# Moving a matmul kernel's squares, weight steps and first products between engines and slots

## The chip, the cores and the metric

One core of one Trainium2 chip runs the whole kernel as one launch. The metric is device time in microseconds (us), from the start to the end of one execution; the kernel before is shown with the median of three runs. The profile is of one execution. Its engines are PE (TensorE's matmuls), PEld (its weight loads), DVE (VectorE), ACT (ScalarE), POOL (GpSimd) and SP (SyncE, which issues the transfers here). Each engine works through its own queue in order; between engines there are only semaphores.

## The reference

Three layers, one behind the other: attention over a local window and a few global positions, a soft mixture of eight experts, and a feed-forward layer whose activation is a squared relu.

```python
def _attn_ref(q, k, v, n_global, n_local):        # batch 4, heads 8, sequence 768, head size 64
    ...
    scores = np.where(keep, scores, -1000000000.0)  # local window or global position
    ...
    return np.matmul(a, v)

def _moe_ref(x, phi, w1, w2):                      # 3072 tokens, width 512, 8 experts of 4 slots
    logits = x @ phi
    d = softmax over tokens; slot_input = d.T @ x
    for e in range(E):
        slot_out[e] = np.maximum(slot_input[e] @ w1[e], 0.0) @ w2[e]
    c = softmax over slots
    return c @ slot_out

def _moe2_ref(x, w_in, w_out):                     # 512 -> 2048 -> 512
    r = np.maximum(x @ w_in, 0.0)
    return (r * r) @ w_out
```

(The two softmax lines stand in words; the reference subtracts the maximum, takes exp and divides by the sum.)

## The kernel before

**Order.** The program is written with a manual schedule: every engine runs its instructions in the order in which the code emits them, so moving a line of code moves the instruction in its engine's queue. The file's names `V`, `G`, `nc.scalar`, `nc.tensor` and `nc.sync` are DVE, POOL, ACT, PE and SP. A tile with `bufs=2` is a ring of two buffers: the third user waits until the first is read. PSUM tiles are banks of 128x512 float32, and a wait on one is for the whole bank. `warm(n, ...)` issues n small matmuls whose result nobody reads.

**Stages.** Attention and routing run in units until about 172 us. The tail of routing (L714 to L796) works on the last two chunks of tokens, K and L: it updates the running sums `rden` and `acc`, turns the last weights (`pd`, copied to `db`), and ends with `slotZ`, the input of the experts. `w1_of` (L819) and `w2_of` (L923) stream the experts' weights through PE, the latter into one bank `pSO`. Between the experts `spread_T` and `spread_ev` (L884 to L889) turn a quarter of the combine weights `c_tok` on PE and store it by ACT and DVE in `cst`, in two halves. Then `pSO` is copied to `SO`, turned (`pst`, `soT`) and multiplied by the first part of w_in (`pu`, L1293), which gives `U0`: the tokens' combine and w_in are one product from here on, `cst` x `U`.

**The feed-forward layer.** The 2048 inner columns come in five parts of WIDTHS = 256, 384, 384, 512, 512, counted q = 0 to 4, and the 3072 tokens in ND = 6 blocks of 512, counted d. For parts 0 to 3 one loop goes over q, d and four steps m, each step the place of one block of 128 output rows; k = 4d + m counts the 24 steps of a part. A step emits, in this order: a number of background steps for the next part's weights, one first product `h` of the next block with its `gate` (L1055, L1043 to L1049), and the second products of this block (L1075, L1076, L1084), whose sum DVE adds into the output accumulator (L1089). A second product needs a high and a low part of the square: `gate` takes the relu on ACT (L1043), the exact square, by DVE from the bank or, with `own`, by ACT from the relu (L1045 or L1047), the rounded square on ACT (L1048) and their difference, the low part, on POOL (L1049; on DVE for the last block of q = 3). Its tile `rg` is on the ring of two `e`, the `h` banks on the rings `h` and `k` of two.

**Background steps.** They convert float64 words of the weights to float32 (L932 on ACT, L933, L934 and L937 on DVE), multiply w_in by the experts' sum (`make_u`, L1016 and L1024), and for the last part (`conv_last`) make seven sums of blocks with their high parts on ACT (L1002) and low parts on DVE and POOL (L1008). `total` and `room` (L1329) deal them out: for the last part `total` = 30 steps over `room` = 18 slots.

**The fifth part** (q = 4) forms pairs of blocks and multiplies them in seven products P1 to P7 (`pair`, L1208 to L1211) instead of eight. Its inner values y11, y12, y22 and y21 (`hy` on PE, `ry` = relu on ACT, squares `yt`), differences of them (L1161, DVE) and the high (ACT, L1148 or L1150) and low (POOL or DVE, L1156) parts `yop` are emitted by `y_steps` at slots of a table; slots below zero of the first pair fall into the steps k = 17 to 23 of q = 3, two each, and slot n from 0 on stands behind the n-th group of a pair. The products run as groups P1, P1, P5, P5, P6, P6, P3, P3, P7, P7 and so on, one per 128 rows.

**The start of the feed-forward layer** (`gemm1_first`): the first block's products for 256 tokens are made separately for the two halves k of the 256 columns, both in one bank, with warm matmuls behind them, then `gemm2_first` begins.

## Time and profile before

| | us |
|---|---|
| median of three runs (512.21, 512.89, 512.85) | 512.85 |
| the profiled execution, as timed | 513.21 |
| its span, first to last instruction | 511.4 |
| PE busy in the span (98%) | 500.3 |
| DVE busy (77%) | 391.9 |
| ACT busy (66%) | 335.3 |
| POOL busy (31%) | 158.1 |

The mean granted clock of TensorE is 0.999 of full speed. A row of the timeline shows an instruction's start, its duration, the line, the tiles (out<-in), and in brackets how long the engine was idle before it and what ended that. The rows of successive matmuls overlap: a 128x512 matmul is shown with 0.39 us while the next starts 0.23 us behind it, so PE's busy share says little about short waits, and starts are to be compared.

### The profile page before, as it was taken

Reading aid. Unit: us, or ns where it says so; the run is one execution under the profiler, and the core shown is the slowest. Engines: PE = TensorE matmul, PEld = TensorE weight load, DVE = VectorE, ACT = ScalarE, POOL = GpSimd, SP = SyncE. Lnnn points to the kernel's source line nnn. Section 1 sums busy time; section 2 is a strip of 40 time slices with the busy share of each in tenths; the row PEclk is TensorE's granted clock in tenths of the full one; section 3 lists DMA queues with packets and bytes.
Section 4 is the critical chain, followed back from the end, with each engine's and each line's share of the span. In section 5 each row is a group of like instructions: output and inputs, shape, how many; then the busy total and the mean of one; then the engine's idle time right before and its main releaser. Section 6 shows DMA issues by size and latency. Waiting matters only on the chain.

```text
span 511.4 us, 9819 instructions
## 1 busy us (share of the span) xinstructions
PE 500.3 (98%) x3517; PEld 382.0 (75%) x3517; DVE 391.9 (77%) x925; ACT 335.3 (66%) x840; POOL 158.1 (31%) x126
## 2 busy tenths in 40 slices
PE   9999999999999999999999999999999998999997
PEld 6777777687777744487887888788887876878785
DVE  7788888787887745688864765788696998579894
ACT  6987877878878402387985856576654566656650
POOL 7000000000000110000454554446644452866691
PEclk9999999999999999999999999999999999999999
DMA  8888999999994799913304040402200000013124
GB/s 278 261 283 295 365 309 326 313 330 314 318 336 139 274 357 420 406 64 126 123 1 164 1 164 2 164 2 67 97 1 1 2 0 1 1 41 124 62 104 164
DMA packets 25975, 86.93 MB, mean 170 GB/s; under 512 B 2882, under 2 KB 5442, under 8 KB 23746
## 3 DMA queue, kind: packets, MB, share of 16 engines
q1 hardware_dynamic: 25776, 86.13, 47.0%
q8 instruction: 29, 0.48, 0.4%
q14 instruction: 24, 0.20, 0.1%
q10 hardware_dynamic: 146, 0.13, 0.1%
HBM read 79.95 MB, written 6.29 MB: 169 GB/s over the span
## 4 chain that ended last, share of the span: by engine, by line
PE 53%; DVE 8%; ACT 1%; issue 0%; DVEq 0%; ACTq 0%
PE acc L1075 10%; PE acc L1076 10%; PE acc L1084 10%; PE pSO L923 3%; PE h L1055 3%; DVE rg L1047 1%; PE b2P L1211 1%; PE b2P L1208 1%; PE b2P L1209 1%; PE b1P L1211 1%; PE b0P L1211 1%; DVE oacc_p L1089 1%; PE b1P L1208 1%; PE b0P L1208 1%; PE b1P L1209 1%; PE b0P L1209 1%
## 5 line engine op out<-in xcount | busy, mean ns | idle before, releaser
L1075 PE MATMUL acc<-g,w 128*128 128x512 f32 x280 | 109.1, 390 | 0.0
L1076 PE MATMUL acc<-g,w 128*128 128x512 f32 x280 | 109.0, 389 | 0.0
L1049 POOL TENSOR_TENSOR g<-rg,g 128x512 fp32r<-128x512 f32 x56 | 75.4, 1352 | 81.8 <-DVE rg L1047 26.5
L263 ACT ACTIVATE sm<-sm,nm 128x256 f32<-128x256 f32 (+1 forms) x192 | 92.7, 487 | 1.3 <-DVE nm L248 1.3
L1084 PE MATMUL acc<-g,w 128*128 128x512 f32 x280 | 75.5, 389 | 0.0
L1043 ACT ACTIVATE rg<-h 128x512 f32<-128x512 f32 (+1 forms) x73 | 43.1, 591 | 44.0 <-PE h L1055 33.9
L248 DVE CUSTOM_DVE_ANT_0 sm<-s,mask 128x256 f32<-128x256 f32 (+1 forms) x192 | 66.8, 397 | 1.9 <-ACT sm L263 1.2
L1076 PEld LDWEIGHTS acc<-g,w 128*128 128x128 f32 x280 | 52.6, 188 | 11.0
L1084 PEld LDWEIGHTS acc<-g,w 128*128 128x128 f32 x280 | 52.6, 188 | 11.0
L1075 PEld LDWEIGHTS acc<-g,w 128*128 128x128 f32 x280 | 52.6, 188 | 10.7
L235 PE MATMUL s<-raw 64*128 64x256 f32 (+1 forms) x384 | 52.9, 397 | 0.0
L1089 DVE TENSOR_TENSOR oacc_p<-acc,oacc_p 128x512 f32<-128x512 f32 x48 | 32.4, 686 | 22.7 <-PE acc L1084 22.7
L673 POOL TENSOR_TENSOR lh<-lh 128x256 f32<-128x256 f32 x1 | 0.7, 731 | 158.4 <-PE pt L274 158.4
L1156 POOL TENSOR_TENSOR yop<-yt,yop 128x512 fp32r<-128x512 f32 x24 | 40.2, 1701 | 25.2 <-ACT yop L1148 9.0
L274 PE MATMUL pt<-con,sm 128*128 128x128 f32 x352 | 45.5, 277 | 1.6 <-ACT pT L280 1.6
L1048 ACT ACTIVATE g<-rg 128x512 fp32r<-128x512 f32 (+1 forms) x73 | 45.4, 621 | 1.6
L291 PE MATMUL o<-pT,v 128*64 128x128 f32 x704 | 44.2, 276 | 0.0
L274 PEld LDWEIGHTS pt<-con,sm 128*128 128x128 f32 x352 | 38.6, 141 | 7.3 <-ACT pT L280 2.8
L291 PEld LDWEIGHTS o<-pT,v 128*64 128x64 f32 x704 | 37.9, 137 | 6.9 <-ACT sm L263 2.1
L235 PEld LDWEIGHTS s<-raw 64*128 64x128 f32 x384 | 32.1, 194 | 14.6 <-DMA v<-in_vx 6.8
L1047 DVE SCALAR_TENSOR_TENSOR rg<-h,rg 128x512 f32<-128x512 f32 (+1 forms) x49 | 32.9, 674 | 9.6 <-ACT rg L1043 9.5
L263 ACT ACTIVATION_READ_ACCUMULATOR sm<-sm,nm 128x1 f32 x192 | 37.0, 193 | 0.0
(289 smaller groups left out, 880.0 us busy)
## 6 DMA issues: line engine op xcount, KB each, us to landing
w<-in_w SPq DMA_DIRECT2D x40, 512.0 KB, 6.6
raw<-in_qk SPq DMA_DIRECT2D x32, 384.0 KB, 5.3
w<-in_w SPq DMA_DIRECT2D x5, 2048.0 KB, 10.0
v<-in_vx SPq DMA_DIRECT2D x32, 256.0 KB, 4.3
raw<-in_qk SPq DMA_DIRECT2D x16, 320.0 KB, 5.1
win<-in_w_in SPq DMA_DIRECT2D x2, 2048.0 KB, 7.9
wout<-in_w_out SPq DMA_DIRECT2D x2, 2048.0 KB, 8.0
out_x<-oacc_p SPq DMA_DIRECT2D x15, 256.0 KB, 2.0
```

Source lines behind the costliest of these rows:

```text
L235: nc.tensor.matmul(sc[hh][:, tt, 0:n, :], lhsT=r[r0 : r0 + D, tt, :], rhs=rhs, start=True, stop=True)
L248: V.tensor_tensor_reduce(out=sm[:, j, 0:n, :], in0=sc[hh][:, tt, 0:n, :], in1=m[:, 2:3, :] if n == 1 else m[:, 0:2, :], scale=-QK_SCALE, s ...
L263: nc.scalar.activation(sm[:, j, 0:n, :], sm[:, j, 0:n, :], AF.Exp, bias=nm[:, j : j + 1], scale=-1.0, accum_out=chunk_sums(i // NPR)[:, tt ...
L274: nc.tensor.transpose(pp[tt][:, hh, c, :], sm[:, 2 * tt + hh, c, :], ident)
L291: nc.tensor.matmul(o[hh * D : hh * D + D, tt, :], lhsT=v[:, c * 3 if tt == 0 else 1 + c, hh * D : hh * D + D], rhs=pT[:, 2 * tt + hh, c, : ...
L1043: nc.scalar.activation(r, ph, AF.Relu)
L1048: nc.scalar.activation(g2[:, 0, js, cs], r, AF.Square)
L1049: (low or (G if q else V)).tensor_tensor(g2[:, 1, js, cs], g, g2[:, 0, js, cs].bitcast(F32), op=ALU.subtract)
L1075: nc.tensor.matmul(pa, lhsT=whi[:, j, ms], rhs=ghi[:, j, :], start=j == 0, stop=False)
L1076: nc.tensor.matmul(pa, lhsT=wlo[:, j, ms], rhs=ghi[:, j, :], start=False, stop=False)
L1084: nc.tensor.matmul(pa, lhsT=whi[:, j, ms], rhs=glo[:, j, :], start=False, stop=j == J - 1)
L1156: eng.tensor_tensor(lo[:, c], yt[y][:, c], hi[:, c].bitcast(F32), op=ALU.subtract)
```

## The change

It has six places.

1. `gate` of the part q = 3 takes the exact square on ACT for the column blocks j > 0, as the parts 1 and 2 do: 18 instructions (three of four column blocks, six token blocks) leave DVE's queue for ACT's.
2. The 30 background steps for the last part are dealt over `room` = 16 slots, not 18.
3. In the fifth part P6's high part moves from slot 0 to -1 and its low part from slot 2 to 1.
4. The first block's two column halves get a bank each in `gemm1_first`.
5. `SO` is copied by ACT in one instruction; the transpositions of the last eighth of the combine weights (`pc3_1`) move from the stream of w2 to behind `pc3_0`, into the bank that `pSO` leaves.
6. In the routing tail, `rden`'s first update becomes two POOL instructions further ahead; the transpositions `pd` of chunk L and their copy come ahead of the warm matmuls and of the product `pr`; `ps` is copied by ACT.

```diff
--- before.py
+++ after.py
@@ -716,6 +716,8 @@
     nc.tensor.transpose(pd[:, 0:P], dT[:, 0:P], ident)
     db = post.tile([P, 4, NS], F32, tag="db", name=f"db{K}")
     nc.scalar.copy(db, pd[:, 0:P].rearrange("p (t s) -> p t s", s=NS))
+    G.tensor_tensor(rden, rden, foK, op=ALU.mult)
+    G.tensor_tensor(rden, rden, dnK, op=ALU.add)
     xbL = post.tile([P, 2, DM], F32, tag="xT", name=f"xb{L}", bufs=2)
     px = bank(f"px{L}_0", True)
     turned(px, xL, 0)
@@ -734,8 +736,6 @@
     pS = bank(f"pS{K}")
     for t in range(4):
         nc.tensor.matmul(pS[t * NS : t * NS + NS, :], lhsT=db[:, t, :], rhs=(xb9 if t < 2 else xbK)[:, t % 2, :], start=True, stop=True)
-    idle = bank("idle2")
-    warm(3, con, idle)
     mxL, nmL = small("rmaxL"), small("nmL")
     V.tensor_reduce(mxL, pq[:, 0:TB], axis=AX.X, op=ALU.max)
     V.scalar_tensor_tensor(nmL, mxL, -1.0, pm[:, 0:1], op0=ALU.mult, op1=ALU.min)
@@ -745,9 +745,15 @@
     nc.scalar.activation(foL, nmK, AF.Exp, bias=nmL, scale=-1.0)
     dT = post.tile([P, TB], F32, tag="dT", name=f"dT{L}")
     nc.scalar.activation(dT, pq[:, 0:TB], AF.Exp, bias=nmL, scale=1.0, accum_out=dnL)
-    V.scalar_tensor_tensor(rden, rden, foK, dnK, op0=ALU.mult, op1=ALU.add)
     V.tensor_tensor(rden, rden, foL, op=ALU.mult)
     V.scalar_tensor_tensor(acc, acc, foK, pS, op0=ALU.mult, op1=ALU.add)
+    pd = bank(f"pd{L}")
+    for t in halves:
+        nc.tensor.transpose(pd[:, t * NS : t * NS + NS], dT[0:NS, t * P : t * P + P], ident[0:NS, 0:NS])
+    idle = bank("idle2")
+    warm(3, con, idle)
+    db = post.tile([P, 4, NS], F32, tag="db", name=f"db{L}")
+    nc.scalar.copy(db[:, 0:2, :], pd[:, 0 : 2 * NS].rearrange("p (t s) -> p t s", s=NS))
     mk.release()
     att.release()
 
@@ -763,12 +769,7 @@
         tc.mark_branch_hint_location("dense", hint="LikelyTaken", engines=[mybir.EngineType.PE, mybir.EngineType.DVE, mybir.EngineType.Activation, mybir.EngineType.Pool, mybir.EngineType.SP])
         pr = bank("pr")
         nc.tensor.matmul(pr[:, 0:1], lhsT=si4, rhs=rden, start=True, stop=True)
-        pd = bank(f"pd{L}")
-        for t in halves:
-            nc.tensor.transpose(pd[:, t * NS : t * NS + NS], dT[0:NS, t * P : t * P + P], ident[0:NS, 0:NS])
         warm(2, con, idle)
-        db = post.tile([P, 4, NS], F32, tag="db", name=f"db{L}")
-        nc.scalar.copy(db[:, 0:2, :], pd[:, 0 : 2 * NS].rearrange("p (t s) -> p t s", s=NS))
         rd = small("om")
         V.tensor_scalar(rd, pr[:, 0:1], dnL, EPS, op0=ALU.add, op1=ALU.add)
         V.reciprocal(rd, rd)
@@ -784,7 +785,7 @@
         for kc in range(4):
             nc.tensor.matmul(pv[kc // 2][:, kc * NS : kc * NS + NS], lhsT=acc[:, kc * P : kc * P + P], rhs=sdO, start=kc % 2 == 0, stop=False)
         ps = post.tile([P, TB], F32, tag="lh", name="ps")
-        V.tensor_copy(ps, pS[:, 0:TB])
+        nc.scalar.copy(ps, pS[:, 0:TB])
         z = slotZ.rearrange("p (e r) -> p e r", r=ZS)[:, :, 0 : 4 * NS].rearrange("p e (k s) -> p e k s", s=NS)
         for c in halves:
             for h in halves:
@@ -1053,18 +1054,18 @@
             return
         ph = fps.tile([P, 2 * TB], F32, tag="k" if (q, d) == (QL - 1, ND - 1) else next(hk), name=f"h{q}_{d}_{j}", bufs=2)
         nc.tensor.matmul(ph, lhsT=wq[q]["U"][:, j * P : j * P + P], rhs=cst[:, d * 2 * TB : d * 2 * TB + 2 * TB], start=True, stop=True)
-        gate(q, g_of(q, d), j, slice(0, 2 * TB), ph, ex.tile([P, 2, 2 * TB], F32, tag="e", name=f"rg{q}_{d}_{j}", bufs=2), q in (1, 2) and j > 0, V if (q, d) == (QL - 1, ND - 1) else None)
+        gate(q, g_of(q, d), j, slice(0, 2 * TB), ph, ex.tile([P, 2, 2 * TB], F32, tag="e", name=f"rg{q}_{d}_{j}", bufs=2), 0 < q < QL and j > 0, V if (q, d) == (QL - 1, ND - 1) else None)
 
     def gemm1_first(n):
-        ph = fps.tile([P, 2, TB], F32, tag=next(hk), name=f"h0_0_0_{n}", bufs=2)
+        phs = [fps.tile([P, 2, TB], F32, tag=next(hk), name=f"h0_0_{k}_{n}", bufs=2) for k in range(1 if n else 2)]
         for k in range(2):
-            nc.tensor.matmul(ph[:, k, :], lhsT=wq[0]["U"][:, k * P : k * P + P], rhs=cst[:, n * TB : n * TB + TB], start=True, stop=True)
+            nc.tensor.matmul(phs[-1 if n else k][:, k, :], lhsT=wq[0]["U"][:, k * P : k * P + P], rhs=cst[:, n * TB : n * TB + TB], start=True, stop=True)
             if n == 0 and k == 0:
                 warm(4, con, idle)
         rg = ex.tile([P, 2, 2, TB], F32, tag="e", name=f"rg0_0_{n}", bufs=2)
         cs = slice(n * TB, n * TB + TB)
         for k0, k1 in ((0, 1), (1, 2)) if n == 0 else ((0, 2),):
-            gate(0, g_of(0, 0), slice(k0, k1), cs, ph[:, k0:k1, :], rg[:, :, k0:k1, :])
+            gate(0, g_of(0, 0), slice(k0, k1), cs, phs[-1 if n else k0][:, k0:k1, :], rg[:, :, k0:k1, :])
 
     def gemm2_hi(q, d, m):
         ghi = g_of(q, d)[:, 0, :, :]
@@ -1167,7 +1168,7 @@
             step(slot_, square, y, k)
         for y, k, x0, x1, slot_ in (("t1", 2, "y12", "y11", -6), ("t2", 0, "y22", "t1", -3), ("t3", 4, "y22", "y12", -2), ("t4", 2, "y21", "t2", 3)):
             step(slot_, diff, y, k, x0, x1)
-        for name, y, s0, s1, eng in (("P1", "y11", -9, -7, G), ("P5", "t1", -3, -1, G), ("P6", "t2", 0, 2, V), ("P3", "y22", -2, 1, G),
+        for name, y, s0, s1, eng in (("P1", "y11", -9, -7, G), ("P5", "t1", -3, -1, G), ("P6", "t2", -1, 1, V), ("P3", "y22", -2, 1, G),
                                      ("P7", "t3", 2, 5, G), ("P2", "y21", 1, 3, G), ("P4", "t4", 6, 8, V)):
             step(s0, high, name, y)
             step(s1, low, name, y, eng)
@@ -1258,10 +1259,6 @@
         if e == 1:
             for _ in conv_in(0):
                 pass
-        if e == 2:
-            pc = pp_of("pc3_1")
-            spread_T(3, 1, pc)
-            spread_ev(3, 1, pc)
         if e == 3:
             for c in conv_out(0):
                 for _ in c:
@@ -1275,8 +1272,7 @@
     pu = [bps.tile([P, 512], F32, tag=f"pu{j}", name=f"pu0_{j}")[:, 0:P] for j in range(WIDTHS[0] // P)]
     for h in range(2):
         spread_T(2, h, pp[h])
-    nc.scalar.copy(SO[:, 0 : 2 * P], pSO[:, 0 : 2 * P])
-    V.tensor_copy(SO[:, 2 * P : 4 * P], pSO[:, 2 * P : 4 * P])
+    nc.scalar.copy(SO, pSO)
     spread_ev(2, 0, pp[0])
     for kc in range(4):
         nc.tensor.matmul(pst[kc // 2][:, kc % 2 * P : kc % 2 * P + P], lhsT=SO[:, kc * P : kc * P + P], rhs=si4, start=True, stop=True)
@@ -1287,12 +1283,16 @@
     wq[0]["U"] = U0
     spread_T(3, 0, pc)
     spread_ev(3, 0, pc)
+    pc = bps.tile([P, 512], F32, tag="so", name="pc3_1")
+    spread_T(3, 1, pc)
     for c0 in range(0, WIDTHS[0], P):
         c = slice(c0, c0 + P)
         for kc in range(4):
             nc.tensor.matmul(pu[c0 // P], lhsT=soT[:, kc, :], rhs=f0[:, kc, c], start=kc == 0, stop=kc == 3)
         nc.scalar.copy(U0[:, c], pu[c0 // P])
         V.scalar_tensor_tensor(U0[:, c], U0[:, c].bitcast(F32), odd, pu[c0 // P], op0=ALU.mult, op1=ALU.add)
+        if c0 == 0:
+            spread_ev(3, 1, pc)
     bps.release()
     wps.release()
 
@@ -1326,7 +1326,7 @@
         q, d = i // ND, i % ND
         if d == 0:
             bg = background(q + 1)
-            total, room = 5 * (WIDTHS[q + 1] // P) + (10 if q + 1 == QL else 7), 4 * (ND - 1) - (2 if q + 1 == QL else 1)
+            total, room = 5 * (WIDTHS[q + 1] // P) + (10 if q + 1 == QL else 7), 4 * (ND - 1) - (4 if q + 1 == QL else 1)
         for m in range(4):
             k = 4 * d + m
             for _ in range((k + 1) * total // room - k * total // room):
```

On ACT, around steps k = 17 to 19 of q = 3 (rg3_5_j is the tile of the gate of block 5, column block j; ry11 and ry12 are relus of the fifth part). Before:

```order
L1043 ACTIVATE rg3_5_1_11916<-h3_5_1_11914 128x512
L1048 ACTIVATE g1_10196<-rg3_5_1_11916 128x512
L1043 ACTIVATE rg3_5_2_11947<-h3_5_2_11945 128x512
L1048 ACTIVATE g1_10196<-rg3_5_2_11947 128x512
L1141 ACTIVATE ry11_0_11921<-hy11_0_0_11922 128x512
L1141 ACTIVATE ry11_0_11921<-hy11_0_1_11924 128x512
L1043 ACTIVATE rg3_5_3_11970<-h3_5_3_11968 128x512
L1048 ACTIVATE g1_10196<-rg3_5_3_11970 128x512
L1144 ACTIVATE yt_11980<-ry11_0_11921 128x1024
L1141 ACTIVATE ry12_1_11975<-hy12_1_0_11976 128x512
```

The same stretch of ACT's queue in the changed kernel:

```order
L1044 ACTIVATE rg3_5_2_11948<-h3_5_2_11946 128x512
L1046 ACTIVATE rg3_5_2_11948<-rg3_5_2_11948 128x512
L1049 ACTIVATE g1_10197<-rg3_5_2_11948 128x512
L1142 ACTIVATE ry11_0_11922<-hy11_0_0_11923 128x512
L1142 ACTIVATE ry11_0_11922<-hy11_0_1_11925 128x512
L1044 ACTIVATE rg3_5_3_11971<-h3_5_3_11969 128x512
L1046 ACTIVATE rg3_5_3_11971<-rg3_5_3_11971 128x512
L1049 ACTIVATE g1_10197<-rg3_5_3_11971 128x512
L1145 ACTIVATE yt_11981<-ry11_0_11922 128x1024
L1142 ACTIVATE ry12_1_11976<-hy12_1_0_11977 128x512
```

Each gate now holds a third ACT instruction, the square of L1046, and ry12's relu stands behind one more of them per gate.

On DVE, at the start of the first pair of the fifth part (b0P100 and b0P110 are P1's banks, b0P500 and b0P510 P5's, yop3 holds P6's parts). Before:

```order
L1191 TENSOR_TENSOR oacc0_10151<-b0P100_12082,oacc0_10151 128x512
L1191 TENSOR_TENSOR oacc0_10151<-b0P110_12092,oacc0_10151 128x512
L1191 TENSOR_TENSOR oacc1_10152<-b0P500_12109,oacc1_10152 128x512
L1156 TENSOR_TENSOR yop3_12064<-yt_11980,yop3_12064 128x1024
L1191 TENSOR_TENSOR oacc1_10152<-b0P510_12121,oacc1_10152 128x512
```

The same stretch in the changed kernel:

```order
L1192 TENSOR_TENSOR oacc0_10151<-b0P100_12084,oacc0_10151 128x512
L1192 TENSOR_TENSOR oacc0_10151<-b0P110_12093,oacc0_10151 128x512
L1157 TENSOR_TENSOR yop3_12065<-yt_11981,yop3_12065 128x1024
L1192 TENSOR_TENSOR oacc1_10152<-b0P500_12111,oacc1_10152 128x512
L1192 TENSOR_TENSOR oacc1_10152<-b0P510_12122,oacc1_10152 128x512
```

P6's low part stands ahead of the add of P5's first group, no longer behind it.

On PE, between the experts and the first product (pc3 are the transpositions of the last quarter, pu0 the product for U0). In the changed kernel:

```order
L1278 MATMUL pst0_10101<-con_63,hZ_2944 128x128 x2
L1278 MATMUL pst1_10102<-con_63,hZ_2944 128x128 x2
L885 MATMUL pc3_0_10100<-con_63,cr3_10001 128x128 x3
L885 MATMUL pc3_1_10127<-con_63,cr3_10001 128x128 x3
L1291 MATMUL pu0_0_10103<-hZ_2944,soT_9933 128x128 x4
L1291 MATMUL pu0_1_10104<-hZ_2944,soT_9933 128x128 x4
L1062 MATMUL h0_0_0_0_10155<-cu_9934 128x256
```

Before, the row of pc3_1 stood inside the stream of w2, behind expert 2, and not here.

## Rows read from the trace of the kernel before

**Rows 1.** Timeline of PE at its four waits; columns: start, duration, instruction, idle before.

```profile
420.75 0.50 PE L1136 MATMUL hy<-cu 128*128 128x512 f32 x1 [0.91 <-DVE rg L1047]
433.05 0.50 PE L1136 MATMUL hy<-cu 128*128 128x512 f32 x1 [1.39 <-ACT ry L1141]
...
451.09 0.39 PE L1208 MATMUL b0P<-yop,xs 128*128 128x512 f32 x1
451.32 0.39 PE L1209 MATMUL b0P<-yop,xs 128*128 128x512 f32 x1
452.47 0.50 PE L1211 MATMUL b0P<-yop,xs 128*128 128x512 f32 x1 [0.77 <-DVE yop L1156]
...
474.26 0.50 PE L1211 MATMUL b1P<-yop,xs 128*128 128x512 f32 x1 [0.64 <-DVE yop L1156]
```

**Rows 2.** Busy time by stretch: PE, PEld, DVE, ACT, POOL, granted clock, DMA.

```profile
340.00:368.00 28.00, 28.00 (x125) 23.20 (x124) 21.84 (x28) 17.67 (x32) 18.35 (x14) 1.00 0.21 75
394.00:412.00 18.00, 18.00 (x81) 14.88 (x81) 17.34 (x25) 10.99 (x19) 6.79 (x5) 1.00 0.01 1
```

**Rows 3.** Groups of DVE from 394 to 432: count, busy us, mean ns, idle before.

```profile
L1047 DVE SCALAR_TENSOR_TENSOR rg<-h,rg 128x512 f32<-128x512 f32 x12 | 8.2, 680 | 0.1
L1008 DVE TENSOR_TENSOR xs<-winf,xs 128x512 fp32r<-128x512 f32 x2 | 3.3, 1638 | 0.0
```

**Rows 4.** Timeline of DVE, end of the fourth part.

```profile
424.33 1.77 DVE L1008 TENSOR_TENSOR xp<-winf,xp 128x512 fp32r<-128x512 f32 x1
...
429.41 0.69 DVE L1049 TENSOR_TENSOR g<-rg,g 128x512 fp32r<-128x512 f32 x1
```

**Rows 5.** Timeline of ACT, end of the fourth part.

```profile
425.17 0.60 ACT L1043 ACTIVATE rg<-h 128x512 f32<-128x512 f32 x1 [1.71 <-PE h L1055]
...
427.54 1.08 ACT L1141 ACTIVATE ry<-hy 128x512 f32<-128x512 f32 x2 [1.11 <-DVE g L1049]
430.19 0.60 ACT L1043 ACTIVATE rg<-h 128x512 f32<-128x512 f32 x1 [1.57 <-DVE g L1049]
430.82 0.63 ACT L1048 ACTIVATE g<-rg 128x512 fp32r<-128x512 f32 x1
431.36 1.04 ACT L1144 ACTIVATE yt<-ry 128x1024 f32<-128x1024 f32 x1
432.40 1.08 ACT L1141 ACTIVATE ry<-hy 128x512 f32<-128x512 f32 x2
```

**Rows 6.** Timeline of DVE and ACT, fifth part.

```profile
444.46 1.06 ACT L1144 ACTIVATE yt<-ry 128x1024 f32<-128x1024 f32 x1 [3.15 <-DVE slotZ L1161]
...
447.67 0.69 DVE L1191 TENSOR_TENSOR oacc<-b0P,oacc 128x512 f32<-128x512 f32 x1 [0.67 <-PE b0P L1211]
...
450.09 2.33 DVE L1156 TENSOR_TENSOR yop<-yt,yop 128x1024 fp32r<-128x1024 f32 x1
...
493.35 1.22 DVE L1156 TENSOR_TENSOR yop<-yt,yop 128x1024 fp32r<-128x1024 f32 x1
```

**Rows 7.** Timeline of PE and ACT, experts' second weights to first products.

```profile
205.52 0.55 PE L884 MATMUL pc<-con,cr 128*128 128x128 f32 x3
206.00 0.64 PE L923 MATMUL pSO<-w,hZ 128*32 128x512 f32 x4
...
219.99 0.38 ACT L1043 ACTIVATE rg<-h 128x256 f32<-128x256 f32 x1 [0.85 <-PE h L1061]
...
221.41 0.39 PE L1238 MATMUL acc<-g,w 128*128 128x256 f32 x1
221.75 0.38 PE L1236 MATMUL acc<-g,w 128*128 128x256 f32 x1
...
222.30 0.39 PE L1238 MATMUL acc<-g,w 128*128 128x256 f32 x1
```

**Rows 8.** Timeline of PE and DVE, tail of routing.

```profile
179.60 0.64 PE L782 MATMUL pS<-xb,db 128*32 128x256 f32 x8
...
179.20 0.21 DVE L773 TENSOR_SCALAR om<-pr,dnL 128x1 f32<-128x1 f32 x1
```

## Prediction

> **What bounds the kernel now.** I read the chain that ended last first: it lies on PE nearly everywhere, and only between 394 and 433 us does it run over DVE and then ACT. So the question is where PE waits, and busy time hides that. I therefore compared the starts of successive matmuls. Two of them normally start 0.23 us apart while each row lasts 0.39 us (at 451.09 and 451.32, [rows 1]). A wait that shows as idle time x thus costs x + 0.16. From 223 us to the end four waits stand out [rows 1]: 0.91, 1.39, 0.77 and 0.64 us idle, so 1.07, 1.55, 0.93 and 0.80 us lost, 4.35 in all. The rest of the layer runs at the pace of its matmuls. The first wait is for DVE's square reading an `h` bank, the second for ACT's relu of y12, the third and fourth for P6's low part on DVE. All further gains of this change must come from the stretch before 223 us.
>
> **Fourth part: squares and weight steps.** DVE is full from 394 us on (17.34 of 18 us) while ACT has 10.99 [rows 2]. Between 394 and 432 DVE makes 12 squares of 0.68 us [rows 3]; three are of column block 0, nine move, 6.1 us. The weight work also comes sooner: it ended with the subtraction at 424.33 [rows 4], dealt to the steps k = 16 and 17, and now belongs to step 15; a step is 13 matmuls of 0.23, 2.95 us. That instruction ends at 426.1; six of the nine squares stand ahead of it (4.1 us), and some 3 us of its two steps can be used before DVE has to wait for sums from PE. So DVE's backlog should be gone by about 419. First consequence: the bank that stopped PE at 420.75 is now read by ACT's relu alone, or earlier by a square of column block 0, since the rings `h` and `k` also swap places (one more bank is drawn at the layer's start). I count this wait, 1.07, as gone.
>
> The second wait sits behind a chain on ACT: the third gate of the last block, the relus of y11, the fourth gate, the square of y11, the first relu of y12 [rows 5]. Before, ACT stood idle in it 1.11 and 1.57 us for DVE's low parts. Now those two waits shrink, but each gate has one more square of 0.63. Worked through with PE 1.07 earlier: the third gate's relu starts at 425.17 - 1.07 = 424.10; relu 0.60 and two squares of 0.63 end at 425.96; y11's relus (1.08) at 427.04; the low part on DVE (0.69, [rows 4]) is done by 426.7, so it no longer holds the fourth gate, which ends at 428.90; square of y11 (1.04) 429.94; first relu of y12 (half of 1.08) 430.48. PE wants that bank at 433.05 - 1.55 - 1.07 = 430.43. With a semaphore's delay I leave 0.1 to 0.3 us of the 1.55 and take 0.3. **Fourth part: 2.62 - 0.3 = 2.3 us.** Bounds: 2.6, and, if ACT is also late for reasons of its own in the steps before (a ring of two `rg` tiles ties each relu to POOL's low part two gates back), 1.0.
>
> The Trainium skill ("ScalarE: Activation LUTs", Rules for kernel authors) says to put multiplication on VectorE, not on ScalarE. The rows here price both alike, 0.68 against 0.63 us; by the rule the move would cost ACT more than it frees, and I give that no weight.
>
> What hides the 18 added squares is ACT's idle time: parts 1 and 2 already run with `own`, and in 340 to 368 ACT is busy 17.67 of 28 us with all of PE's time filled [rows 2]. If that cover fails, each late gate costs up to 0.6 us.
>
> **P6's parts.** The high part moves into the 3.15 us in which ACT waited for DVE (at 444.46, [rows 6]), so it costs nothing, and everything behind it on ACT comes 1 us sooner. The low part now follows the add at 447.67 (0.6 us until the next can start): it starts near 448.3 instead of 450.09 and, at the slow 2.33 us, ends at 450.6. PE needs it at 451.55. The wait is gone with 0.9 to spare; in the second pair the order is the same. What is queued behind it on DVE, P5's adds, slips about 1 us; the next user of P5's banks is P3's group, four groups of 1.36 us on. In the third pair the same low part took 1.22 us (at 493.35, [rows 6]) and held nobody. **Gain 1.7**, bounds 0.9 (only half of it, if another add or difference slides in front) and 1.73.
>
> The difference between 1.22 and 2.33 is POOL being at work. The Trainium skill ("SBUF — State Buffer", Who interferes with whom) calls the port pair of DVE and GpSimd an exclusive lock for a whole instruction; the rows agree, and the sum above uses the slow row.
>
> **Start of the layer.** The three transpositions in the stream of w2 cost the 0.48 us from 205.52 to 206.00 [rows 7]. At their new place they follow three of the same kind; the row's 0.55 for three, less its 0.22 of overlap with the next matmul, is 0.33. But their ACT and DVE stores now stand between the two halves of `U0`, and I estimate 0.1 of delay to the second half from that. Net 0.1. The separate banks: ACT's first relu waited 0.85 us for the second half's matmul (at 219.99, [rows 7]), since both wrote one bank; now it starts 0.7 us sooner, and two late starts should close: 221.75 is 0.34 us behind 221.41 where half of 0.23 is due for 256 columns, and 222.30, which also waited for a part of the second half, I put at the same 0.2: 0.4 together. The one copy of `SO` is a little longer on ACT than a half, but six transpositions cover it; if not, it costs 0.1. **Gain 0.5**, bounds 0 and 0.75.
>
> **Tail of routing.** PE waited for `db` before 179.60 [rows 8]; with the copy sooner the product pS can start when the warm matmuls end, 0.2 us sooner. But pr moves behind the warm matmuls, so DVE's division, at 179.20 behind the update of `acc`, is not sooner, and pv needs it. **Gain 0.1**, bounds -0.2 (the division 0.2 later) and +0.25. POOL's two small instructions have 3 us of cover.
>
> **Sum.** 2.3 + 1.7 + 0.5 + 0.1 = 4.6 us. Against the profiled execution's own 513.21: 508.6. That execution lay 0.36 above the median of the three runs, so on their scale 508.25, call it **508.3 us**. The bounds added up run from 513.21 - 5.3 = 507.9 to 513.21 - 1.7 = 511.5, or 507.5 to 511.1 on the runs' scale.
>
> **Rivals.**
>
> *ACT takes DVE's place.* The squares move one load from a full engine to one with a tight chain. If ACT's chain of rows 5 does not shorten, the second wait stays and the first is all that falls: 2.62 - 1.07 = 1.55 less gain, 509.9. For it: the chain above leaves no slack at all. Against: ACT's two waits there, 2.7 us, were for DVE, and only three squares, 1.9 us, are added.
>
> *The change does not reach P6.* The low part slips behind another DVE instruction or its high part comes late; the waits of 0.93 and 0.80 stay: 510.0. Against it: the order shows it right behind P1's second add, and ACT's hole is three times its length.
>
> *Slower: DVE's weight steps run into PE.* 30 steps now fall on 16 slots. From k = 8 to 15 DVE has some 27 us of work for 24 us of PE: about 20 of weights (38 us from 394 to 432, less 8.2 of squares [rows 3], 12 adds of 0.6 and four low parts of 0.69), and 9 adds and 2 squares. It starts with a lead of one step. The adds of the second products stand behind conversions, and PE has three `acc` banks: when an add is over one group (2.9 us) late, PE stops. It decides on POOL: L1008 takes 1.64 us on average [rows 3], where the same subtraction of the same size took 0.69 at 429.41 [rows 4]. If the other dozen instructions of the weight steps that read two tiles ran so slowly too, that would be some 10 us more, of which the three banks absorb 4; PE would lose about 6, and with the 2.3 of P6, start and tail kept, the time is 512.85 - 2.3 - 2.6 + 6 = 514. By the skill's lock rule above this is just what would happen if POOL ran without pause. Against it: POOL is busy 6.79 of 18 us there [rows 2], and by my schedule the add that matters most, of block 3's first rows, is done 0.4 us before its bank is wanted.
>
> **How the numbers follow.** Forecast (all four waits go or nearly go) 0.66, at 507.5 to 509.5; ACT takes over 0.13, at 509.5 to 510.5; P6 not reached 0.06, 510; a mixture in which DVE or POOL gives most back, 512 to 513, 0.08; slower 0.07, 514. The range that leaves out 2 in 10 at most runs from 507.3 to 510.8. A measurement of this kernel tells about 0.2%, 1.0 us, from no change: faster than 511.8 holds the first three cases, 0.85; within 0.2% the mixture, 0.08; slower 0.07.
>
> **What would show it.** Right: no PE row with more than 0.3 us idle before `hy` or before P6's L1211; the last L1008 on DVE before 420 us of the old scale; P6's low part on DVE right behind P1's second add; L1236 and L1238 at the layer's start 0.11 us apart. Wrong: idle time of PE before an `acc` matmul in k = 12 to 17 released by DVE L1090, or `hy` released by ACT L1142 for over 0.5 us; a granted clock below 1.00 between 178 and 183 us, where the warm matmuls have moved.

## The result: 0.9% less, about as forecast, by terms that partly cancel

| | us |
|---|---|
| before, beside it, median of four runs (512.21 to 513.45) | 512.87 |
| changed kernel, median of four runs (506.95 to 508.98) | 508.26 |
| ratio, with its 95% interval | 0.9907 (0.9893 to 0.9921) |
| profiled execution of the changed kernel, as timed | 508.98 |
| its span (before 511.4) | 506.9 |

Line numbers of the changed kernel are mostly one higher than before (L1136 is L1137, L1156 is L1157); those of the start of the layer differ more. Busy time by engine over the span, from the page of the changed kernel:

```profile
PE 499.1 (98%) x3517; PEld 382.5 (75%) x3517; DVE 380.0 (75%) x904; ACT 345.1 (68%) x859; POOL 159.9 (32%) x128
```

DVE lost 12 us and ACT gained 10, which says that the squares moved, not what it is worth. That is read where PE waited before [rows 1]. Timeline of PE in the changed kernel at the same four places (start, duration, instruction; a bracket would show idle time before):

```profile
420.03 0.61 PE L1137 MATMUL hy<-cu 128*128 128x512 f32 x2
...
430.45 0.80 PE L1137 MATMUL hy<-cu 128*128 128x512 f32 x2
431.09 0.40 PE L1076 MATMUL acc<-g,w 128*128 128x512 f32 x1
...
449.28 0.62 PE L1212 MATMUL b0P<-yop,xs 128*128 128x512 f32 x2
...
470.13 0.62 PE L1212 MATMUL b1P<-yop,xs 128*128 128x512 f32 x2
```

No bracket is left. Two matmuls at full pace take 0.61 or 0.62; the pair at 430.45 takes 0.80, and this is all that remains of the 1.39 us at 433.05. The second stretch of [rows 2], in the same columns:

```profile
394.00:412.00 18.00, 18.00 (x81) 14.92 (x80) 17.83 (x23) 12.74 (x24) 7.61 (x6) 1.00 0.01 2
```

From 394 to 412 DVE is even fuller than before, 17.83 against 17.34 of 18 us, since the weight steps come sooner; ACT has 12.74 instead of 10.99. ACT's chain behind it, against [rows 5]:

```profile
424.53 0.60 ACT L1044 ACTIVATE rg<-h 128x512 f32<-128x512 f32 x1 [0.86 <-PE h L1056]
...
427.48 0.60 ACT L1044 ACTIVATE rg<-h 128x512 f32<-128x512 f32 x1 [0.19 <-PE h L1056]
...
430.12 1.06 ACT L1142 ACTIVATE ry<-hy 128x512 f32<-128x512 f32 x2
```

Its idle times of 1.11 and 1.57 us for DVE's low parts are gone; it now waits for PE, and y12's relu starts at 430.12 instead of 432.40. And DVE, with the last weight step's last instruction (before at 424.33, [rows 4]) and P6's low part (before at 450.09, [rows 6]):

```profile
415.79 1.16 DVE L1009 TENSOR_TENSOR xp<-winf,xp 128x512 fp32r<-128x512 f32 x1
...
445.40 0.69 DVE L1192 TENSOR_TENSOR oacc<-b0P,oacc 128x512 f32<-128x512 f32 x1 [0.67 <-PE b0P L1212]
446.01 1.97 DVE L1157 TENSOR_TENSOR yop<-yt,yop 128x1024 fp32r<-128x1024 f32 x1
```

So both late parts went as forecast. The start of the layer did not (changed kernel; compare [rows 7]):

```profile
219.73 0.56 DVE L890 TENSOR_TENSOR cu<-pc,cu 64x384 fp32r<-64x384 f32 x1
...
220.24 0.38 ACT L1044 ACTIVATE rg<-h 128x256 f32<-128x256 f32 x1
...
220.32 0.35 DVE L1293 SCALAR_TENSOR_TENSOR cu<-cu,odd,pu 128x128 fp32r<-128x128 f32 x1
...
220.82 0.35 PE L1062 MATMUL h<-cu 128*128 128x256 f32 x1 [0.16 <-DVE cu L1293]
...
222.37 0.28 PE L1237 MATMUL acc<-g,w 128*128 128x256 f32 x1
222.49 0.28 PE L1238 MATMUL acc<-g,w 128*128 128x256 f32 x1
```

The banks did their work: ACT's first relu has no wait, and the `acc` products follow each other in 0.12 us. But PE now waits for U0's second half, whose last step on DVE (220.32) stands behind the subtraction of the moved `pc3_1` (219.73).

**Where the 4.5 us of span went.** Adding, over each stretch, by how much PE's starts exceed their usual distance: 3.11 us between 420 and 440 became 0.30 (2.81 gained); the two waits at P6, with the late start behind each, 2.02 became 0.03 (2.0); a small wait of 0.2 near 500 is gone too. The stretch from the end of the tail of routing to the first product of the second part's weights stayed as long as it was (52.61 before, 52.66 now). And this execution was already 0.54 us late at the end of the tail of routing (181.71 against 181.17), 0.30 of it from its first product that waits for data, at 2.57 instead of 2.27 us, where nothing was changed:

```profile
2.57 0.56 PE L143 MATMUL n_p<-n,one 1*128 1x4 f32 x2 [0.25 <-DVE n L138]
```

In the profiles of the experiments below the same place at the tail's end lies between 180.53 and 181.28, also where the tail has the changed order, so the half microsecond is scatter between executions.

### The profile page after: what moved, and what is told of

The parts are those of the page before. It is cut to its first block, busy times and chain, and to the rows that moved or that the text cites. A ratio compares the mean times of both kernels' runs of the same rounds, so it can differ in the third digit from the quotient of the medians.

```text
span 506.9 us, 9822 instructions
## 1 busy us (share of the span) xinstructions
PE 499.1 (98%) x3517; PEld 382.5 (75%) x3517; DVE 380.0 (75%) x904; ACT 345.1 (68%) x859; POOL 159.9 (32%) x128
## 4 chain that ended last, share of the span: by engine, by line
PE 61%; DVE 0%; issue 0%; ACT 0%; DVEq 0%
PE acc L1076 13%; PE acc L1077 13%; PE acc L1085 13%; PE h L1056 3%; PE pSO L924 3%; PE b2P L1212 1%; PE b2P L1209 1%; PE b2P L1210 1%; PE b1P L1212 1%; PE b0P L1210 1%; PE b1P L1209 1%; PE b0P L1212 1%; PE b1P L1210 1%; PE b0P L1209 1%; PE hy L1137 1%; PE pre L820 1%
## 5 line engine op out<-in xcount | busy, mean ns | idle before, releaser
L1050 POOL TENSOR_TENSOR g<-rg,g 128x512 fp32r<-128x512 f32 x56 | 77.2, 1387 | 76.6 <-DVE rg L1048 19.1
L1157 POOL TENSOR_TENSOR yop<-yt,yop 128x512 fp32r<-128x512 f32 x24 | 41.5, 1759 | 23.8 <-PE hy L1137 11.9
L280 ACT COPY pT<-pt 128x512 f32<-128x512 f32 x46 | 26.5, 578 | 15.3 <-PE pt L274 15.1
```

The costliest lines, as they stand in the source:

```text
L1050: (low or (G if q else V)).tensor_tensor(g2[:, 1, js, cs], g, g2[:, 0, js, cs].bitcast(F32), op=ALU.subtract)
L1157: eng.tensor_tensor(lo[:, c], yt[y][:, c], hi[:, c].bitcast(F32), op=ALU.subtract)
```

## The experiments

### One part alone

Four kernels, each the kernel before with one part of the change. The fourth part's edit:

```diff
-    ... q in (1, 2) and j > 0, V if ...
+    ... 0 < q < QL and j > 0, V if ...
-    ... room = ..., 4 * (ND - 1) - (2 if q + 1 == QL else 1)
+    ... room = ..., 4 * (ND - 1) - (4 if q + 1 == QL else 1)
```

> Kernel before with the fourth part's edit alone (ScalarE squares its own relu for the second, third and fourth 128 channels of each tile of the fourth part; weight steps of that part two slots sooner); the chain's tail keeps its order. Theory of the prediction: the waits at 420.75, 430 to 433 and their neighbours go, 2.3 us, and the two of P6 (451.09, 474.26) stay: 510.6 us. Rival 'the pieces hold each other up' (the time saved in the fourth part is eaten by the tail, since P6 then meets the same busy engines sooner): under 1 us, 512 or more. In the trace: no start of the products y11, y12, y21, y22 of the fourth part later than 0.3 us after its neighbour's pace, and the waits at P6 as long as before, 1.0 and 0.9 us.

Measured 509.83, ratio 0.9948 (0.9934 to 0.9961), 2.6 us less. In its timeline of PE the wait at P6 stands as before (0.77, [rows 1]):

```profile
448.72 0.50 PE L1211 MATMUL b0P<-yop,xs 128*128 128x512 f32 x1 [0.76 <-DVE yop L1156]
```

P6 alone:

```diff
-("P6", "t2", 0, 2, V)
+("P6", "t2", -1, 1, V)
```

> Kernel before with P6's two steps one slot sooner and nothing else. Theory of the prediction: P6's high half goes into ScalarE's idle time ahead of t1's and its low half to VectorE behind P1's second add, so both waits of TensorE there (1.05 and 0.94 us) go: 1.7 us less, 511.1. Rival 'the move does nothing without the sooner fourth part' (the tail starts with VectorE still behind, so the low half is as late as before): 512.5 to 512.9, with the wait at 451.09 still over 0.7 us.

Measured 510.43, ratio 0.9963 (0.9949 to 0.9976), 2.0 us less by the medians; the waits of the fourth part stay within 0.02 us (0.91 and 1.39 before; PE's timeline):

```profile
420.17 0.50 PE L1136 MATMUL hy<-cu 128*128 128x512 f32 x1 [0.89 <-DVE rg L1047]
...
432.47 0.50 PE L1136 MATMUL hy<-cu 128*128 128x512 f32 x1 [1.39 <-ACT ry L1141]
432.80 0.39 PE L1075 MATMUL acc<-g,w 128*128 128x512 f32 x1
```

So the two late parts don't lean on each other. The last two rows also show what the sum had left out: 0.33 us lie between them where 0.23 is the rule, so a wait costs one more 0.11 in the start behind it.

The banks alone (`phs`, as in the diff of the change):

> Kernel before with one PSUM bank for each half of the chain's first tile, and nothing else. Theory of the prediction: ScalarE's first relu no longer waits until the second half's product is written, the first relu starts 0.7 us sooner and the two late starts of acc at 221.75 and 222.30 go: 0.4 us less, 512.4 (a tenth of a per cent, hardly above the spread of the times; the trace decides). Rival: the first products then wait for VectorE's U0 instead, and the late starts stay at their 0.43 us together: 512.9.

Measured 512.03, ratio 0.9989 (0.998 to 0.9998), 0.4 us less by the medians. ACT's timeline, against 219.99 with 0.85 idle in [rows 7]:

```profile
219.03 0.38 ACT L1043 ACTIVATE rg<-h 128x256 f32<-128x256 f32 x1
...
219.85 0.38 ACT L1043 ACTIVATE rg<-h 128x256 f32<-128x256 f32 x1
```

The moved transpositions and the one copy of the sum, alone:

```diff
-        if e == 2:
-            pc = pp_of("pc3_1")
-            spread_T(3, 1, pc); spread_ev(3, 1, pc)
...
-    nc.scalar.copy(SO[:, 0 : 2 * P], ...); V.tensor_copy(SO[:, 2 * P : 4 * P], ...)
+    nc.scalar.copy(SO, pSO)
...
+    pc = bps.tile([P, 512], F32, tag="so", name="pc3_1")
+    spread_T(3, 1, pc)            # behind pc3_0; stores between the halves of U0
```

> Kernel before with the one copy of the experts' sum on ScalarE and the transpositions of pc3_1 (with their two stores) moved out of the w2 products to behind them, and nothing else. In the trace of the changed kernel TensorE waited 1.2 us, in 2 waits, for the last w2 weights to land. Theory A, formed from that: the transpositions taken out of the w2 products gain nothing, since the last weights land no sooner, and in the block behind they cost their 0.33 us and, by the stores ahead of U0's second half on VectorE, another 0.3 us at the second half's first product: first acc product 0.5 to 0.8 us later behind the first w2 product than before (before 20.92 us), time 513.0 to 513.6. Theory B, the prediction's: the 0.48 us taken out is gained and 0.33 paid back: that distance 20.7 to 20.9 us, time 512.8.

Measured 513.22, ratio 1.0015 (1.0006 to 1.0024): this part costs 0.77 us (0.31 to 1.23). Theory A's time came, and the block behind w2 is longer. The distance from the first transposition behind the w2 products to the first product of `make_u`, both as starts in each kernel's timeline of PE, tells the block apart from all before it:

| kernel | first transposition | first product of make_u | distance |
|---|---|---|---|
| before | 214.95 | 233.78 | 18.83 |
| banks alone | 214.74 | 233.01 | 18.27 |
| moved transpositions alone | 215.22 | 234.72 | 19.50 |
| changed kernel | 215.48 | 234.37 | 18.89 |
| changed kernel, stores later (below) | 214.06 | 233.12 | 19.06 |
| changed kernel without moved part and tail (below) | 215.16 | 233.43 | 18.27 |

The banks give 0.56, the moved part takes 0.67, and the changed kernel has the difference. Where the 0.67 arises can be read from starts in PE's timeline, each counted from the last w2 product:

| start | before | moved transpositions alone | later by |
|---|---|---|---|
| first `pst` | 1.23 | 1.28 | 0.05 |
| first transposition of `pc3_0` | 2.13 | 2.27 | 0.14 |
| first product for U0 (`pu`) | 2.45 | 2.93 | 0.48 |
| second half's first `h` | 5.15 | 5.76 | 0.61 |
| first product of make_u | 19.36 | 20.02 | 0.66 |

0.14 us are lost ahead of `pc3_0`, before PE comes to a moved transposition; the edit's only other part there is the one copy of the sum, which was not run alone. The three transpositions cost 0.34. The stores between the halves of `U0` add some 0.13.

The tail of routing alone:

```diff
-    idle = bank("idle2"); warm(3, con, idle)
...
+    pd = bank(f"pd{L}")           # turned and copied ahead of the branch
+    ...
+    idle = bank("idle2"); warm(3, con, idle)
```

> Kernel before with the other order in the tail of the routing alone (the last block's transpositions and its copy ahead of the branch, the denominator's step on GpSimd, the sum's copy on ScalarE). Theory of the prediction: 0.1 us less (from 0.25 less to 0.2 more), 512.4 where before is 512.5. Theory from the trace of the changed kernel: nothing, since the product pr stands behind the warming products there and the division that follows it starts 0.14 us later, which takes the gain back: from the first pd transposition's end of the block before, the first w1 product comes after the same 4.1 us as before, and the time is 512.3 to 512.7.

Measured 512.56 beside 512.68, ratio 0.9998 (0.9989 to 1.0007): nothing that can be measured. From the start of the transposition (or, before, of the warm matmuls) behind the last pS of chunk K to the first w1 product it took 4.09 us before and 4.07 here. The reason stands in the changed kernel's rows, of PE and of DVE:

```profile
179.96 0.64 PE L783 MATMUL pS<-xb,db 128*32 128x256 f32 x8
...
179.09 0.75 DVE L749 SCALAR_TENSOR_TENSOR acc<-acc,fo,pS 128x512 f32<-128x512 f32 x1 [0.29 <-PE pS L738]
179.90 0.22 DVE L774 TENSOR_SCALAR om<-pr,dnL 128x1 f32<-128x1 f32 x1
```

The product pS does start 0.2 sooner against what lies before it, but the division (179.90; before 179.20 at [rows 8], in an execution 0.56 earlier) is 0.14 later, and the next products need it. The part's four edits were not run one by one.

The parts by themselves add up to 2.64 + 2.04 + 0.44 - 0.75 + 0.12 = 4.5 us by the medians; the whole change gave 4.6.

### What ends the w2 products

The changed kernel with six transpositions put back among the w2 products, into a bank that nobody reads:

```diff
+        if e == 2:
+            pad = pp_of("pad")
+            for _ in range(2):
+                spread_T(3, 1, pad)
```

> The changed kernel with six transpositions, into a bank that nobody reads, put among the w2 products behind the third expert's, where before had the three of pc3_1 (0.59 us with their turn of the weights; six are about 0.92 us). Theory A (the landing of the last weights ends the w2 products): TensorE's waits for weights there (1.2 us in the changed kernel) shrink by about as much, the last w2 product comes 14.2 to 14.6 us behind the first as without them (14.28 us), and the time stays at 507.9 to 508.6. Theory B (TensorE's own work ends them): 15.2 us, and 0.9 us more, 509.2.

Measured 507.91 (507.74 to 508.63), no more than the changed kernel's 508.26, where theory B has 509.2. Waits of PEld between 199 and 217 us (engine, tile and line, releaser: us in all, times, longest), the changed kernel's first:

```profile
PEld pSO L924 <- DMA w<-in_w: 1.2, 2, 0.8
```

and this kernel's:

```profile
PEld pSO L924 <- DMA w<-in_w: 0.2, 1, 0.2
```

The added work took the place of waiting for weights. The last w2 product came 14.66 us behind the first, a little more than expected, but the same distance scatters from 14.09 to 14.76 among kernels in which this stretch is as before. What sets it can be read from the trace of each kernel: when the last of the w2 weights landed, and when the last w2 product started (differences of unrounded times).

| kernel | transpositions among w2 | last weights landed | last w2 product | behind it |
|---|---|---|---|---|
| before | 3 | 213.92 | 214.43 | 0.50 |
| changed kernel | 0 | 214.45 | 214.95 | 0.50 |
| this kernel | 6 | 213.44 | 213.94 | 0.50 |
| third spread moved too (`k_best2`, below) | 9 | 212.72 | 214.20 | 1.47 |

The ten other kernels, with three transpositions or none, have 0.50 as well. Theory A is shown for up to six transpositions: the landing of the last weights ends the stretch, and what PE does there before is free. That holds for the kernel before too, although its waits list no landing: there PE's work fills the time until the weights come. With nine the room is used up, and PE ends 0.97 us later than the landing would have it.

### Better places for the start of the layer

The changed kernel with `spread_ev(3, 1, pc)` one place later:

```diff
-        if c0 == 0:
+        if c0 == P:
             spread_ev(3, 1, pc)
```

> The changed kernel with the two stores of pc3_1 behind U0's second half instead of between the halves. If VectorE's subtraction ahead of U0's second half is what makes the second half's first product wait (0.33 us at 220.82 in the changed kernel), that wait goes and the time is 0.3 us less, 507.9 where the changed kernel has 508.26; the 0.43 us that the transpositions themselves and the later copies add stay. Rival: the store's copy on ScalarE then stands ahead of the second tile's relu and gives the wait back there: no change, and a late start of 0.2 to 0.4 us at the first acc products.

Measured 507.84 (507.23 to 508.3), not apart from the changed kernel. In PE's timeline the wait at the second `h` is gone, and a late start has come up behind it, as the rival said:

```profile
219.24 0.36 PE L1062 MATMUL h<-cu 128*128 128x256 f32 x1
...
221.27 0.28 PE L1238 MATMUL acc<-g,w 128*128 128x256 f32 x1
221.58 0.39 PE L1239 MATMUL acc<-g,w 128*128 128x256 f32 x1
```

By the table of distances above the block is 0.17 longer, not shorter. Neither of the two places that were tried is free; the wait only moved.

The fourth part, P6 and the banks without the rest (the edits of the three kernels above together; called `k_best`):

> Kernel before with the fourth part's edit, P6's slots and the chain's banks, and without the other three (the experts' sum stays two copies, the transpositions of pc3_1 stay among the w2 products, the routing's tail stays). Theory: the terms add, since each removes a wait of TensorE at a place of its own: 2.65 + 2.04 + 0.45 us below before, 507.3, and 0.75 us below the changed kernel, which pays that for the moved transpositions. Rival: moved transpositions and banks belong together (with separate banks their cost is covered), and the changed kernel is as fast, 508.0 to 508.3.

Measured 507.28 (507.1 to 507.87), ratio 0.9893 (0.9878 to 0.9909), 5.4 us below before: the terms add. It is the best version found. Its interval overlaps the changed kernel's; that it is 0.6 to 0.8 us better rests on the block's 18.27 against 18.89 and on the cost of the moved part measured alone.

On top of that, the six transpositions of the third spread moved into the w2 products as well, with one copy of the sum (`k_best2`):

```diff
+        if e == 4:
+            for h in range(2):
+                spread_T(2, h, pp[h]); spread_ev(2, h, pp[h])
...
-    for h in range(2):
-        spread_T(2, h, pp[h])
+    spread_T(3, 0, pc)
-    nc.scalar.copy(SO[:, 0 : 2 * P], ...); V.tensor_copy(SO[:, 2 * P : 4 * P], ...)
+    nc.scalar.copy(SO, pSO)
```

> The kernel k_best, with one copy of the experts' sum on ScalarE and with the six transpositions of the third spread (and their stores) moved into the w2 products, behind the fifth expert's, where TensorE waits for weights at the end anyway. Theory A (the last weights' landing ends the w2 products, with room of 0.5 to 1 us left beside pc3_1): the block behind loses 0.71 us of transpositions and gets back up to 0.5 us of waiting for the copy of the sum: 0.2 to 0.5 us less than k_best, 506.8 to 507.1. Theory B (no room left with pc3_1 there already): the last w2 product comes 0.7 to 0.9 us later behind the first, the time is k_best's or 0.3 us more, 507.3 to 507.6.

Measured 508.19, ratio 0.9911 (0.9896 to 0.9926): neither theory's time, 0.9 worse than the kernel it builds on. Its timeline of PE behind the w2 products:

```profile
214.72 0.55 PE L884 MATMUL pc<-con,cr 128*128 128x128 f32 x3
215.49 1.16 PE L1283 MATMUL pst<-con,hZ 128*128 128x128 f32 x8 [0.23 <-ACT hZ L1281]
```

With three transpositions instead of six to fill the time, PE waits for ACT's copy of `pSO`: `pst` starts 1.29 us behind the last w2 product, and before it was 1.24 with all six in between. The six were free where they stood, too. From the last w2 product to `make_u` it takes 18.98 here (214.20 to 233.18) and 18.79 in the kernel it builds on, so 0.2 of the 0.9 lies in the block. The rest fits the table of the section on w2: with nine transpositions the last w2 product comes 1.47 us behind the landing of its weights instead of 0.50, and no wait of PEld for weights is left. So theory B has the mechanism here, PE's own work ends the stretch, though its price was set too low; 0.97 and 0.2 together are more than the 0.9 between the medians, but the landing itself scatters by some tenths between executions.

### The fourth part taken apart

ScalarE's squares alone, with 18 slots:

> Kernel before with ScalarE's own squares in the fourth part alone; the weight steps keep their 18 slots. Theory 'the squares carry it': nine squares of 0.68 us leave VectorE between 394 and 432 us, so its backlog is gone with or without sooner steps, and most of the fourth part's 2.65 us comes: 510.0 to 510.6 where before is 512.5 to 512.7. Theory 'both are needed' (the last weight step still ends at about 424 us of before, ahead of the gates of y11's and y12's tiles): the wait at 420.75 goes, since ScalarE's relu alone reads that bank, 1.07 us, and the one at 430 to 433 stays at over 0.7 us: 511.2 to 511.6.

Measured 509.97, ratio 0.9945 (0.9932 to 0.9959). The squares carry it, as the first theory had it: the excess of PE's starts between 420 and 440 is 0.25 us, the same as with both edits (0.25 in the kernel with the fourth part's whole edit).

The sooner weight steps alone, 16 slots:

> Kernel before with the fourth part's weight steps two slots sooner (16 instead of 18) and VectorE's squares left where they were. Theory 'the squares carry it': VectorE is full from 394 us on, so steps that are dealt out sooner run no sooner; gain under 0.5 us, 512.1 to 512.6, the waits at 420.75 and 433.05 still 0.7 us or more each. Theory 'the steps carry it': as the fourth part's whole edit, 510.0 to 510.4. A loss would be the prediction's slower rival at work (VectorE's weight steps ahead of the adds that free TensorE's acc banks): a wait ahead of an acc product between 400 and 420 us.

Measured 510.61, ratio 0.9961 (0.9948 to 0.9975): 1.8 us less, so steps dealt out sooner do run sooner, against the theory that only the squares count, and both waits at `hy` are gone. But a new wait stands where the prediction's slower rival put it. Timelines of PE, DVE and POOL of this kernel:

```profile
414.65 0.50 PE L1075 MATMUL acc<-g,w 128*128 128x512 f32 x1 [1.03 <-DVE oacc_p L1089]
...
410.41 0.68 DVE L1047 SCALAR_TENSOR_TENSOR rg<-h,rg 128x512 f32<-128x512 f32 x1
...
411.61 1.79 DVE L1008 TENSOR_TENSOR xs<-winf,xs 128x512 fp32r<-128x512 f32 x1
413.32 0.68 DVE L1047 SCALAR_TENSOR_TENSOR rg<-h,rg 128x512 f32<-128x512 f32 x1
413.92 1.27 DVE L1089 TENSOR_TENSOR oacc_p<-acc,oacc_p 128x512 f32<-128x512 f32 x2
...
411.26 1.58 POOL L1049 TENSOR_TENSOR g<-rg,g 128x512 fp32r<-128x512 f32 x1 [2.65 <-DVE rg L1047]
```

The add that frees PE's bank (413.92) is late by two squares and by a subtraction of 1.79 us beside POOL. Without the squares ahead of it, in the changed kernel, it is in time. So each of the two edits removes the old waits by itself, and the squares also remove the one that the other brings.

The changed kernel with 12 slots, to see when that mechanism decides:

```diff
-    ... 4 * (ND - 1) - (4 if q + 1 == QL else 1)
+    ... 4 * (ND - 1) - (8 if q + 1 == QL else 1)
```

> The changed kernel with the weight steps of the fourth part dealt to 12 slots instead of 16. The prediction's slower rival, pushed: per slot VectorE then gets 2.5 weight steps instead of 1.9 while it is already full between 394 and 412 us; the adds that free the acc banks and the gates' low parts stand behind them, and TensorE waits ahead of acc or h products between 395 and 420 us: 2 to 5 us more, 510 to 513. If instead the three acc banks and the lead of the steps absorb it, as at 16 slots, the time stays within 0.4 us of the changed kernel's 508.26.

Measured 512.39, ratio 0.9999 (0.999 to 1.0008) against before: the whole gain is lost again, 4.1 us. PE's two waits, and DVE ahead of the second:

```profile
382.50 1.05 PE L1017 MATMUL pu<-winf,soT 128*32 128x512 f32 x2 [1.53 <-DVE winf L938]
...
406.67 0.50 PE L1076 MATMUL acc<-g,w 128*128 128x512 f32 x1 [1.52 <-DVE oacc_p L1090]
...
400.23 2.38 DVE L1005 TENSOR_TENSOR winf<-winf 128x512 f32<-128x512 f32 x2
402.54 1.78 DVE L1009 TENSOR_TENSOR xs<-winf,xs 128x512 fp32r<-128x512 f32 x1
404.25 1.76 DVE L1005 TENSOR_TENSOR winf<-winf 128x512 f32<-128x512 f32 x1
405.94 1.28 DVE L1090 TENSOR_TENSOR oacc_p<-acc,oacc_p 128x512 f32<-128x512 f32 x2
407.13 0.68 DVE L1009 TENSOR_TENSOR xs<-winf,xs 128x512 fp32r<-128x512 f32 x1
```

The add at 405.94 stands behind four weight instructions, 5.7 us. The first wait was not foreseen: with the steps this early, the weights of `make_u` are wanted before DVE has converted them.

## Why the prediction came out right

**Fourth part: right in mechanism, 0.3 to 0.5 short in size.** 2.3 was forecast; 2.64 was measured alone, 2.81 in the trace. The chain on ACT shortened as it was worked through, and a little more: y12's relu was put at 429.94 and starts at 430.12, in an execution that is 0.59 us later by then (first `hy` at 420.03 against 419.44), so 0.4 sooner than worked through. The working had added up durations, where most of ACT's rows overlap the next by some 0.1 us. What was missing is the 0.11 us behind each wait, and one more small late start at 428. The text took the edit's two halves together; the squares alone do it, and the 16 slots on top of them add nothing that could be measured.

**P6: right in mechanism, 0.3 short.** 1.7 forecast, 2.04 measured: again 0.11 behind each of two waits, and the small wait near 500, which was not listed as P6's (it is gone with P6's edit alone and still there with the fourth part's). One reading beside the sum was off: that the low part takes 2.33 us where POOL is at work and 1.22 where it isn't. POOL was at work both times, and what differs is which of the two began first (POOL's timeline before, to compare with DVE's 450.09 and 493.35 in [rows 6]):

```profile
450.05 3.51 POOL L1156 TENSOR_TENSOR yop<-slotZ,yop 128x512 fp32r<-128x512 f32 x2
...
493.63 4.34 POOL L1156 TENSOR_TENSOR yop<-yt,yop 128x512 fp32r<-128x512 f32 x2 [0.76 <-POOL yop L1156]
497.93 2.54 POOL L1156 TENSOR_TENSOR yop<-slotZ,yop 128x512 fp32r<-128x512 f32 x2
```

At 450.09 DVE began behind POOL and took 2.33; at 493.35 DVE began first, took 1.22, and POOL's two took 4.34 instead of 2.54 (beside the second, another DVE instruction that reads two SBUF tiles was at work, from 495.08).

**Start of the layer: wrong, 0.5 forecast; the block's length went from 18.83 to 18.89, and the stretch of w2 got no shorter (14.19 before, 14.28 now).** The banks were right (0.4 forecast, 0.44 and 0.56 measured). The step that failed is the net gain of 0.1 from the moved transpositions, which cost 0.77. First and most, 0.48 us were counted as removed from the w2 stretch because PE was busy there; what was not read is the landing of the last weights, which ends that stretch with the three transpositions or without them. Second, the one copy of `SO` was taken as covered, or 0.1 at worst; the 0.14 us lost ahead of `pc3_0` are most likely its price. The transpositions at their new place (0.33 forecast, 0.34 measured) and the stores between the halves of `U0` (0.1 forecast, 0.13 measured) were right.

**Tail of routing: 0.1 forecast, nothing measured.** The text named the reason itself, the division that is not sooner, and kept 0.1 all the same. The sign of being wrong that it named, a granted clock below 1.00 from 178 to 183 us, did not show: it is 1.00 there in both kernels.

**The sum**, by the medians of the parts alone, was 0.7 too small in the late ones (4.0 forecast, 4.68 measured) and 0.8 too large in the early ones (0.6 forecast, a loss of 0.19 measured); that 4.6 was forecast and 4.61 measured is partly luck. The range's upper end was set by cases that did not come; its bounds on the start (0 to 0.75) did not hold the small loss there (0.06 in the block, 0.31 by the medians of its two parts).

**The rivals.** ACT taking DVE's place left 0.18 us at 430.45 and no more. The slower rival was real as a mechanism: it needs the squares still on DVE (1.03 us idle with 16 slots) or steps still sooner (12 slots), and its price then is 1 to 4 us, not 6. The row that makes it decide is the subtraction beside POOL, as the text said. POOL's and DVE's timelines in the changed kernel show how:

```profile
414.56 1.83 POOL L1050 TENSOR_TENSOR g<-rg,g 128x512 fp32r<-128x512 f32 x1
416.37 1.74 POOL L1009 TENSOR_TENSOR xs<-winf,xs 128x512 fp32r<-128x512 f32 x1
...
414.57 0.68 DVE L1009 TENSOR_TENSOR xp<-winf,xp 128x512 fp32r<-128x512 f32 x1
415.17 0.68 DVE L1090 TENSOR_TENSOR oacc_p<-acc,oacc_p 128x512 f32<-128x512 f32 x1
415.79 1.16 DVE L1009 TENSOR_TENSOR xp<-winf,xp 128x512 fp32r<-128x512 f32 x1
```

DVE's subtraction of two SBUF tiles took 0.68 when it began with POOL's instruction, which then took 1.83 (the same one took 1.28 at 420.57, where it began ahead of DVE's); the next took 1.16, about 0.5 more, ending 0.6 behind the end of POOL's. The add in between, which reads a PSUM bank, took its usual 0.68 beside POOL. The Trainium skill ("SBUF — State Buffer", Who interferes with whom) calls this an exclusive lock that one of the two holds for a whole instruction, while the other blocks; these rows agree with it.

## What to carry to other kernels

Work is free under a transfer that ends the stretch, as long as it fits in the time until the landing: before moving something out of a stream of weights or into it, compare the last landing with the last product, and not the busy share. Here six transpositions fitted and nine did not. Count a wait of PE from start to start, and add the slower start behind it. When several edits go in together, measure each of them alone: here the squares and P6 carried the gain, the banks a tenth of it, the sooner slots and the tail nothing, and the moved transpositions took back 0.77 us, which the total hid.

## What the runs showed of the hardware that was not expected

- A matmul of 512 columns that had to wait starts the next one 0.33 us behind it instead of 0.23 and is shown with 0.50 us instead of 0.39 (432.47 and 432.80 above), at a granted clock of 1.00: 0.11 us for each wait on top of the idle time.
- Two DVE and POOL instructions of 512 columns that meet cost DVE's 0.5 to 1.1 us (0.68 becoming 1.16, 1.78 or 1.79) or POOL's 0.3 to 0.55 (1.28 becoming 1.58 to 1.83), where both read SBUF only. In the two cases above, at 450.09 and 493.35, the one that began second paid.
- The last w2 product starts 0.50 us behind the landing of the last w2 weights in 13 of 14 kernels, with none to six transpositions in between, and 1.47 us behind it with nine.
- The time from the first to the last w2 product varied between 14.09 and 14.76 us among kernels with the same work there, and the end of the routing's tail between 180.53 and 181.71: more than 1 us of the scatter between executions lies ahead of the feed-forward layer.
